# A memory-attention and gating kernel on one core: the spatial weight is loaded first, and the written order is new

## The chip, the core and the metric

The kernel runs on one core of a Trainium2 chip. Five engines work side by side: TensorE (PE, with its weight loads shown as PEld), VectorE (DVE), ScalarE (ACT), GpSimd (POOL) and SyncE (SP), which here issues every DMA. The metric is the device time of one execution in microseconds.

## The reference

Two parts are joined. The first is attention over a small memory, for 8 batches and 8 heads, 576 positions, 64 dimensions and 32 memory slots; the second is a gated feed-forward layer whose gate mixes positions.

```python
a = softmax(phi, axis=positions)            # [B, H, 576, 32]
k_m, v_m = a^T k, a^T v                     # [B, H, 32, 64]
attn = softmax(q k_m^T / 8) ; x = attn v_m  # heads side by side: [B, 576, 512]
h = relu(x @ w_in)                          # [B, 576, 1024]
u, v = h[..., :512], h[..., 512:]
v_n = (v - mean(v)) / sqrt(var(v) + 1e-6)
v_s = w_spatial @ v_n + b_spatial           # mixes the 576 positions
out = (u * v_s) @ w_out                     # [B, 576, 512]
```

All data is float32 except `w_in` and `w_out`, which arrive as 64-bit floats and are decoded on the chip.

## The kernel before, in words

The kernel is a set of small generators, one for each kind of work, and each `yield` ends a step. The string `START` is the written order: each letter takes one step of the generator that it names, so the string alone sets the order of the instructions on every engine (`manual_schedule`, PE, DVE, ACT, POOL and SP). A digit picks the part (a tile or a weight), `*n` repeats, one prime is one batch ahead, and `>` moves on to the next batch.

- `P` loads `phi` and takes its softmax; `K` loads `k` and `v` and forms the two memories (tile `kvm`, then `vmn`, `tv`, `vT`); `Q` loads `q` and transposes it (`tq` in batch 0, `qT` from `q_sb` later); `S` makes the scores and their softmax (`sc`, `sm`, and the transposed result `at` split into a high and a low part `ah`, `al`).
- `M` multiplies `vT` with a half of `w_in` (`mp`, split into `mh`, `ml`); `V` makes a block of `v` and normalizes it (`pv`, `vr`, `st`, `few`, `vh`, `vl`); `U` makes `u` (`pu`); `G` is the spatial product and the gate (`ps`, `g`, `gh`, `gl`); `O` is the last product (`po`, `o`) and the store.
- Weights: `D` loads `w_in` (`load_win`, D1 its v half in four pieces E00 to E11, D0 its u half in two pieces L0 and L1) and `E`/`L` decode it (`decode`: one ACT, one POOL or ACT, one DVE instruction a piece, into `win_sb`); `X` does the same for `w_out` (`raw_out`); `W` loads `w_spatial` and its bias (`w_sb`, `w_rem`, `b_sb`), `T` transposes it (PE tiles `wt`, `wr`) and splits it into `wth` and `wtl` (and `ws`).

A weight load can be held: `hold` (line 194) lets POOL copy one element of a tile that has landed into the buffer that the load will write, so that the DMA behind it starts only when that landing is in. `HOLD` (line 98) names which landing each load waits for: E0 for `k`, E1 for `v`, L0 for E00, L1 for E10 and W for E11. So the loads of the start run `phi`, `q`, `k`, `v`, then the v half of `w_in`, then its u half, and the spatial weight last.

[...] The first batch's products need the decoded v half of `w_in` (`mp` line 711), `ah` and `al`; the first `pv` (line 744) needs all of these; the first `ps` (line 864) needs the normalized blocks and the transposed spatial weight.

Of the kernel before, what the change touches and what calls it, by code (L numbers as in the profile page):

```python
# [17 lines left out]
PSUM = bass.MemoryType.PSUM  # L18

START = """  # L20
    P*4 Q P*4 K D1 P*3 Q P*4 Q P*2 K*4 K1 K Q D1 K Q*2 K*2 D1 K D1 K E0*2 Q D1*2 E1 Q S Q S Q*2 S
# [4 lines left out]
    V0 X0 V4 V1 K' V2 V4*2 V1 X2 P' T4 U3 V2 K' V4 V1 V3 T4 P' G2 V4 T4 U0 X1 Q' U0 G0 V3 P' P'' K'
    Q' U0 K' U1 V2 S V3 V2 V4 K' Q' G2 G0 V2 G2 B U1 P'' K'' V3*2 G0 K' V4 K'*2 V3 V4*2 P''*2 X2 K'
    V4 K'' P'' G0 X3 U1 Q' K' P'' G0*2 P'' G0 G2*2 S' G3 G2 K' X1 G0 G1 P'' X2 P'' S'*3 X3 G1 S' G3
    G2 P'' G0 G2 X2 G1 T2 U1 G0 S' G2 P'' S' P'' G3 G1 G3 P'' M1' M0' L1 S' G1 X3 K''*2 G2 G1 M1'*2
    G1 S' P''*2 Q'' X3 M0' G3 G1 S' Q'' G3 K'' M1' X2 X3 O0 O3 T4 S' X2 S' G3 S' K'' O1 G3 S' M0'  # L30
    S' X3 S' O3 P''' M1' S'*2 M1' P''' O0 G1 O1 S' M0' V1' M0' P''' O3 S' V1' V2' V0' P'''*2 M0'
    V2' U1' O1 K''*2 V1' V0' V2' P''' Q'' U1' O0 V4' K''*2 V2' U0' Q'' V2' P''' V2' K'' P''' V0'
    P''' O2 G1 K'' Q'' V0' U1' V3' U0' V2' K''' O2 U3' V1' V4' P''' K''' P''' U2' V0' U3' S' V1' M0
    X1 V4' U2' K'' K1 U1' V0' Q'' V4' P''' V1' V0' X2 P''' S'' T3 V3' O2 U3' P''' V4' M0'' K''' G3
    V3' O3 V1' S''*2 O1 P''' U0' V4' U2' K''' U2' S'' U3' G3 M1'' M1' U0' S'' V3'*2 S'' K''' V4'*2
    V3' K''' G1' T0 P'''' G1' S'' M0'' G0' V4' G1' Q''' K''' G0' K''' V4' M0' V3' Q''' K''' M1''
    K'''' S'' G0' G1' G0' M1'' S'' G3' G1'*2 G3' P'''' G2' G0' S'' M1'' P'''' G1' G2' G3' S''*2 G2'
    G3' P'''' G0' S''*2 M1'' G2' G0' M0'' G0' S'' G0' S'' P'''' S'' G1' T1 X3 G1' G0' S'' G2' G1'
    P'''' G2'*2 M1 O3' S'' P'''' Q''' O1' G3' M0'' V0'' G3' V0'' K''' G3' S'' G2' V4'' G2' V4'' O0'
    O2 G2' G3' O0 > P''' O0 V1' V4'*2 V3' O2 K'' Q'' O0 P''' O2 G3 Q'' G3 V1' O3 K'' V0' V1' O4 M0'  # L40
    O2 V2' U1' K''' V0' U3' V1' X0 M1' U3' V0' U1' O1 U2' U0' K'' V0' P''' V1' P''' U0' V3' U3'
    P''' V1' U1' O2 O4 V0' V2' O3 P''' Q'' O0 U2' M0'' U0' P''' U1' U0' V1' V2' V3' M0' U3' S''
    K'''*2 P''' M1'' V4' O1 V2' V4' V3' U2' V2' O4 G1' S''*2 U2' V3' S'' V4' M0''*2 O3 V3' G1' M0''
    O1 O4 V3' M0'' G0' V4' S'' V2'*2 P'''' O0 G1' S'' V4'*2 M1'' G1' G0' S'' G0' G1' M1'' G0' G3'
    K''' S''*2 G3' P'''' O1 > Q'' S' G2 G0 G1 S' O4 P''' G2 G0 S' G1 P''' K'' G2 P''' G0 S' G0 G1
    K'' G0 G2 G3 S'*2 K''' G3 P''' K'' S'*2 G0 K'' M1' S' O0 G3 U3' G1 K'' G3*2 G1 Q'' G2 M1' G2 S'
    V1' G2 S' V4' P''' O1 V0' G2 V4' G3 U3' O0 K'' V0' O2 Q'' V0' V1' P''' O3 G3 U3' V3' K'' V1'
    P''' O0 U1' O2 V0' Q''*2 U1' U3' Q'' M0' V1' V0' P''' K'' U0' G3 P''' V4'*2 U0' V4' V0' P''' O1
    V0' U0' G2 U2' O2 U2' V3' U1' V1' K''' V2' V3' U2' O1 V1' O3 S'' P''' V1' O0 P''' M0'' M1'' S''
    U2' V3' Q''' V2' Q''' K''' P''' V4' U0' S S''*2 U1' K''' S'' V3' V2' O3 M1' O0 M0'' G0' M0''  # L50
    K''' V4'*2 S'' V2' M1'' V3' V2' M1'' V3' V2'*2 M0'' G0' G1' G0' V4'*2 G2 K''' G1'*2 O1 G1' M0''
    S' S'' G1' K''' S'' G0'*2 G3' P'''' G0' P'''' G2'*2 S'' G1'*2 P'''' G2' G3' G0' S'' M1'' S''
    G1' S'' G1' G0'*2 O4'' G3' P'''' K''' G2' G3' G1' G0' S'' G2' G3' S'' P'''' M1'' K''' O3' S''
    G3' G2' G3' O2 P'''' O1' S''*3 O4' U1'' S'' G3' V1'' G2' M0'' O0' O3 S'' G2' K'''' V1'' V0''*2
    U1'' O0' V1'' V0'' P'''' V4'' P'''' O3' V4'' K''' V4'' U1'' V1'' O1' V0''*2 Q''' O0' V0''
    U0''*2 Q''' U3'' G3' U3'' V4'' G3' V1'' Q''' G2' V0'' U1'' V4'' V2'' O3' U0'' V1'' K''' U3''
    O1' P'''' K'''' U3'' V2'' Q''' G2' U2'' V4'' O0' V4''*2 O1' K''' V3''*2 V1'' O2' P'''' U2''*2
    K''' O2' P'''' S'' V4'' O4' U2'' S''' U0'' V2'' V3'' V2'' M0''' K'''' S''' V3'' M1''' K''''
    M1'' S''' O4' O2' O3' G1'' G0'' V2'' G1'' G0'' S''' V3'' M0''' P'''' V2'' V3'' P''''*2 S'''*2
    M0''' M1'''*2 V2'' V4'' M1''' P'''' S''' G1'' G0'' V3'' M1''' S''' O4' O1 > S'' P'''' S'' G1'  # L60
    G0' G3' G1' S'' Q''' G1' G0' G1' S'' G3' S'' G0' S'' G3' K'''' P'''' G3' S''*2 G1' P'''' K'''
    G2' M0'' G1' G0'*3 G2' S'' G0' O1 G2'*2 G3' S'' P''''*2 K''' S'' O2 G3' S'' G1' G3' V1''*2
    P'''' K'''' V4'' K''' G2' V0'' M0'' G2' U3''*2 M1'' K''' P''''*2 V0'' Q'''*2 U0'' G3' K''' Q'''
    V4'' P'''' U3'' V4'' G2' V0'' K''' V0'' U0'' Q''' K''' O2' G2' O2' O0' V0'' K''' V0'' V4'' O0'
    V4'' K''' G2' V2'' V3'' O1' V1'' O3' Q''' O2' U3'' U2'' V4''*2 O1' V1'' V0'' P'''' U0'' U1'' O0
    > V3' O0 V1' G3 O3 U0' V1' V3' P''' G2 P''' U1' U2' P''' O1 S'' M1'' V1' V2' V4' U1' V2' S'' O2
    O3 V4' U2' M0' U2' S'' U1' V2'*2 M0'' M1'' V2' P''' K''' M1'' K''' S'' G0' V2' V3' G0' M0'' V3'
    G1' G3 Q''' S'' M0'' V4' S'' M1'' G0' S'' M0'' V3' O0 M1'' P''' G1' S'' V3' G1'*2 G0' S'' G1'
    S'' M0'' Q''' S'' G1'*2 S'' G0' S'' G3'*2 S''*2 G0' S''*2 G0' G3' G2' G0' G2' S''*2 G1' Q'''
    K''' G3' G2'*2 V0'' V2'' G0' V0'' O1 K''' G0' V0'' G1' O3' V2'' U1'' G1' G2' K''' G2' K''' O2'  # L70
    S'' G3'*2 V1'' V0'' G2' Q''' V0''*2 K''' U1'' G2' V4'' U3'' O0' V1'' G3' V4'' G2' U1'' V0''
    V4'' K''' O1' G3' V4'' V2'' V1'' O0' U3'' G2' O1' O0' O2' V4'' U3'' V4'' U1'' V3'' K''' Q'''
    V4'' O4' V4'' S' G3' V4''*2 O2' G3' O1' V3'' O4' U2'' K''' V4'' V1'' O3 O4' U2'' O0' V3'' U0''
    V2'' Q''' V1'' U2'' U0'' V2'' O1 V3'' U3'' V3'' O3' S''' K''' U0'' M0''' S''' U2'' U0'' V3''
    M1''' K''' O3' S''' V1'' M0''' O0' V1'' S''' M1''' V2'' S''' M0''' G2'' G1'' G2'' M1'''*2 S'''
    V2'' S''' M1''' G1'' G0'' V3'' G0'' S''' G0'' S''' M0''' G1'' G0''*2 G2'' S'''*2 G1'' G3'' G0''
    G2'' S''' U1'' G3'' S''' M0''' G0'' S''' O1' O0 > G3' S'' G0' S'' G1' S''*2 G0' G3' G0' U2''
    S'' V1'' G1' U3' G2' G1' S'' G1'*2 G2' V1'' V0'' G1' V3'' G3' U2'' V0'' O2 V3'' V0'' Q'' V0''
    U1'' V0'' V1'' V4'' U1'' V1'' G3' G2' U0'' U3'' V1'' G3' U2''*2 V0'' O1' V1'' U0'' U3'' V0''
    G3' V4''*3 V2'' G2' V4'' U1'' O3' U0'' G3' U0'' V2'' V1'' O3' U3'' O1' O2' V3''*2 O0' V2'' V4''  # L80
    G0'' V4'' V2'' V3'' V4'' G0'' U1'' V4'' O4 V2'' G3' U3'' V2'' V3'' G1'' V2'' G0'' O2' V4'' G1''
    V3'' G3'' G0'' G1'' G0'' G1'' O3 G3'' G2' O1' O3' G2' U0' O0' G2'' G1'' G3'' G0'' G1'' G2''
    G3'' O2' G1'' G2'' O0' G1'' G0'' O1' G0'' G2'' G1'' G0''*2 G3'' G1'' G2''*2 G3'' O4'' O2'
    G2''*2 O0' G3'' O3'' G3'' O3'' O0'' O1'' O1 > G2' O0' O3 > G3 O3 G2 O1 G3 O4 O0 O2 O1 O2 O3 O4
# [901 lines left out]
```

## Time and profile before

| | us |
|---|---|
| time of the kernel, median of 3 runs | 415.3 (414.23 to 415.58) |
| the profiled execution | 416.39 |
| its span, from the first to the last instruction | 414.6 |
| PE busy | 388.7 (94% of the span) |
| DVE busy | 278.7 (67%) |
| ACT busy | 221.6 (53%) |
| POOL busy | 96.0 (23%) |

The page shows PE busy in nearly every slice after the first quarter; its open slices lie at the start and at the very end. The transfers of the start are `phi` of one batch (576 KB), `q`, `k` and `v` (1152 KB each), `w_spatial` (1152 KB and a rest of 144 KB), `w_in` (four pieces of 512 KB, two of 1024 KB) and `w_out` (four of 512 KB).

### The profile page before, as it was taken

How to read it: one execution, taken by the hardware profiler on the slowest of the kernel's cores; microseconds unless marked ns; L12 is line 12 of the kernel's file. 1: busy time of each engine (PE TensorE's matmuls, PEld its weight loads, DVE VectorE, ACT ScalarE, POOL GpSimd, SP SyncE). 2: the span in 40 equal slices, each digit the busy share in tenths (PEclk: the TensorE clock that was granted, in tenths of full speed). 3: DMA queues.
4: the chain of work that ended last, by engine and by line, in shares of the span. 5: the costliest groups of instructions: out<-in, count | busy, mean ns of one | idle time of the engine just before them, and what ended most of it. 6: DMA issues, size and time to landing. Idle time of an engine off the chain costs nothing.

```text
span 414.6 us, 9446 instructions
## 1 busy us (share of the span) xinstructions
PE 388.7 (94%) x3903; PEld 336.5 (81%) x3903; DVE 278.7 (67%) x547; ACT 221.6 (53%) x455; POOL 96.0 (23%) x188
## 2 busy tenths in 40 slices
...
GB/s 300 318 306 304 195 284 197 73 278 27 73 154 227 51 52 154 242 60 134 44 298 2 26 64 129 293 20 149 69 2 0 28 82 22 1 2 25 54 49 101
DMA packets 85758, 50.69 MB, mean 122 GB/s; under 512 B 66194, under 2 KB 70290, under 8 KB 85716
## 3 DMA queue, kind: packets, MB, share of 16 engines
...
q14 instruction: 12, 0.10, 0.1%
HBM read 40.65 MB, written 9.44 MB: 121 GB/s over the span
## 4 chain that ended last, share of the span: by engine, by line
PE 76%; DMA 8%; DVE 6%; SPq 3%; POOL 2%; issue 1%; ACT 1%; DVEq 0%; POOLq 0%; ACTq 0%
PE ps L864 26%; PE po L901 22%; PE pu L828 10%; PE pv L744 9%; DMA kv_sb<-in_v_dram 3%; PE kvm L460 3%; PE mp L711 3%; SPq L516 2%; DMA q_sb<-in_q_dram 2%; DMA w_sb<-in_moe_w_spatial_dram 2%; PE sc L645 2%; DMA raw<-in_moe_w_in_dram 1%; DVE gl L885 1%; POOL raw L225 1%; SPq L448 1%
## 5 line engine op out<-in xcount | busy, mean ns | idle before, releaser
L864 PE MATMUL ps<-wth,vh 128*128 128x288 f32 x256 | 56.8, 302 | 0.1
L864 PE MATMUL ps<-wth,vl 128*128 128x288 f32 x256 | 55.0, 296 | 0.8 <-DVE vl L806 0.8
L864 PE MATMUL ps<-wtl,vh 128*128 128x288 f32 x256 | 54.7, 295 | 0.0
L901 PE MATMUL po<-woh,gl 128*128 128x512 f32 x128 | 50.3, 393 | 1.7 <-DVE gl L885 1.7
L901 PE MATMUL po<-woh,gh 128*128 128x512 f32 x128 | 51.0, 398 | 0.0
L901 PE MATMUL po<-wol,gh 128*128 128x512 f32 x128 | 50.1, 392 | 0.0
L883 ACT CAST gh<-g 128x512 fp32r<-128x512 f32 x32 | 19.6, 618 | 48.1 <-DVE g L877 41.7
L864 PEld LDWEIGHTS ps<-wth,vh 128*128 128x128 f32 x256 | 41.5, 189 | 3.6 <-DVE sm L656 1.1
L864 PEld LDWEIGHTS ps<-wth,vl 128*128 128x128 f32 x256 | 41.1, 188 | 1.1 <-DVE vl L806 1.1
L864 PEld LDWEIGHTS ps<-wtl,vh 128*128 128x128 f32 x256 | 41.2, 188 | 0.0
L789 DVE BATCH_NORM_STATS2 st<-vr 128x6 f32<-128x512 f32 (+1 forms) x40 | 27.2, 679 | 18.8 <-ACT vr L786 18.6
L828 PE MATMUL pu<-ah,mh 128*128 128x288 f32 x128 | 38.5, 301 | 0.2 <-ACT u L837 0.2
L801 ACT ACTIVATE vr<-vr,few 128x512 f32<-128x512 f32 (+1 forms) x40 | 32.0, 814 | 11.2 <-POOL few L796 11.1
L828 PE MATMUL pu<-al,mh 128*128 128x288 f32 x128 | 37.8, 295 | 0.0
L828 PE MATMUL pu<-ah,ml 128*128 128x288 f32 x128 | 37.7, 294 | 0.0
L877 DVE TENSOR_TENSOR g<-u,ps 128x288 f32<-128x288 f32 x64 | 26.9, 443 | 14.4 <-PE ps L864 13.6
L806 DVE TENSOR_TENSOR vl<-vr,vh 128x512 fp32r<-128x512 f32 x32 | 21.8, 682 | 20.9 <-ACT vh L804 20.7
L907 ACT COPY o<-po 128x512 f32<-128x512 f32 x36 | 20.9, 588 | 21.9 <-PE po L901 19.7
L695 POOL CAST ar<-ah 128x128 fp32r<-128x128 f32 x7 | 3.5, 494 | 122.5 <-ACT ah L688 122.5
L792 POOL TENSOR_SCALAR few<-few 128x1 f32<-128x1 f32 (+1 forms) x40 | 10.1, 252 | 93.7 <-DVE few L790 78.6
L786 ACT ACTIVATE vr<-pv 128x512 f32<-128x512 f32 x32 | 19.1, 600 | 21.8 <-PE pv L744 19.6
L901 PEld LDWEIGHTS po<-woh,gl 128*128 128x128 f32 x128 | 24.0, 188 | 7.8 <-DVE gl L885 2.6
...
## 6 DMA issues: line engine op xcount, KB each, us to landing
...
raw_out<-in_moe_w_out_dram SPq DMA_DIRECT2D x4, 512.0 KB, 10.2
```

The costliest lines, as they stand in the source:

```text
L460: nc.tensor.matmul(kvm[r][32 * j : 32 * j + 32], phi_sb[halves[r], j, i, :], kv_sb[halves[r], j, :, i * D : (i + 1) * D], start=(i == 0), ...
L744: nc.tensor.matmul(pv, x[:, r, cs], m[:, r, DM:DFF], start=(n == 0), stop=(n == 5))
L786: nc.scalar.activation(vr, pv, AF.Relu)
L789: nc.vector.bn_stats(st6, vr)
L801: nc.scalar.activation(vr, vr, AF.Identity, bias=sh, scale=rs)
L806: nc.vector.tensor_tensor(vl[:, st, :], vr, vh[:, st, :].bitcast(F32), op=ALU.subtract)
L828: nc.tensor.matmul(pu[hf], m[:, r, cs], a[:, r, at[hf]], start=(r == 0 and n == 0), stop=(r == 1 and n == 2),)
L864: nc.tensor.matmul(ps[hf], a, w[:, hf * HALF : (hf + 1) * HALF], start=(n == 0), stop=(n == len(ops) - 1),)
L877: nc.vector.tensor_tensor(g[:, at], u[:, dt, at], ps[hf], op=ALU.mult)
L883: nc.scalar.copy(hi, x)
L901: nc.tensor.matmul(po, a, w, start=(n == 0), stop=(n == 11))
L907: nc.scalar.copy(o, po)
```

## The change

`w_spatial` (both parts) is issued as the very first transfer and held for nothing; `phi`, `q`, `k` and `v` follow. Holds are moved: E1 is held for the landing of the spatial weight (long in by then), L0 for `v`, L1 for E00, and the first two loads of `w_out` get a hold of their own (X0 for E11, X1 for L00). The string `START` is written anew up to its last batches (the piece behind the last but two `>` is the same). All instructions stay, but for one POOL copy that goes and two that come.

```diff
 START = """
-    P*4 Q P*4 K D1 P*3 Q P*4 Q P*2 K*4 K1 K Q D1 K Q*2 K*2 D1 K D1 K E0*2 Q D1*2 E1 Q S Q S Q*2 S
+    W*2 P*2 T4 T1 P*2 Q K P*4 T0 W P*2 Q T1 Q P*3 Q T4*2 T0 Q T1 P*2 T4 D1 T4 Q T1 Q P T4 T1 K T0
...
-HOLD = {"E0": "k", "E1": "v", "L0": "E00", "L1": "E10", "W": "E11"}
+HOLD = {"E0": "k", "E1": "W", "L0": "v", "L1": "E00", "X0": "E11", "X1": "L00"}
...
     def prepare_out(b, j):
         raw = two.tile([P, 1, 2 * DM], I32, tag="raw_out", name="raw_out")
+        if f"X{j}" in HOLD:
+            hold(raw[0:1, :, 0], HOLD[f"X{j}"])
         nc.sync.dma_start(raw[:, 0], w_out[j * P : (j + 1) * P].bitcast(I32))
...
-        hold(w_sb[0:1, 0, 0:1].bitcast(I32), HOLD["W"])
-        yield
+        if "W" in HOLD:
+            hold(w_sb[0:1, 0, 0:1].bitcast(I32), HOLD["W"])
+            yield
         nc.sync.dma_start(w_sb, w_spatial[0:SM].rearrange("(i p) s -> p i s", i=NI))
+        state["landed", "W"] = w_sb[0:1, 0, 0:1].bitcast(I32)
         yield
```

SP, the start of the program, before (`in_moe_w_in` is `w_in`, and so on):

```order
L333 DMA phi_sb<-in_phi_dram 128x4x288
L534 DMA q_all<-in_q_dram 128x4x576
L375 DMA kv_sb<-in_k_dram 128x4x576
L375 DMA kv_sb<-in_v_dram 128x4x576
L206 DMA raw<-in_moe_w_in_dram 128x1024 x4
L206 DMA raw<-in_moe_w_in_dram 128x2x1024 x2
L266 DMA w_sb<-in_moe_w_spatial_dram 128x4x576
L268 DMA w_rem<-in_moe_w_spatial_dram 64x576
L333 DMA phi_sb<-in_phi_dram 128x4x288
```

and in the changed kernel, at the same place:

```order
L271 DMA w_sb<-in_moe_w_spatial_dram 128x4x576
L274 DMA w_rem<-in_moe_w_spatial_dram 64x576
L339 DMA phi_sb<-in_phi_dram 128x4x288
L540 DMA q_all<-in_q_dram 128x4x576
L381 DMA kv_sb<-in_k_dram 128x4x576
L276 DMA b_sb<-in_moe_b_spatial_dram 2x576
L381 DMA kv_sb<-in_v_dram 128x4x576
L208 DMA raw<-in_moe_w_in_dram 128x1024 x3
L208 DMA raw<-in_moe_w_in_dram 128x2x1024
L208 DMA raw<-in_moe_w_in_dram 128x1024
L208 DMA raw<-in_moe_w_in_dram 128x2x1024
L454 DMA kv_sb<-in_k_dram 128x4x576
```

1296 KB of spatial weight now stand ahead of `phi`, one 1024 KB piece of the u half has passed the last piece of the v half, and the next batch's `k` follows the weights at once.

PE, from the start of the program to the first products of `k`, before:

```order
L343 MATMUL mt_105<-ident,mx 128x128
L352 MATMUL mb_116<-ident,cmb 128x128
L544 MATMUL tq_121<-ident,q_all 128x128 x4
L386 MATMUL kvm_0_0_135<-kv_sb,phi_sb 32x64
L386 MATMUL kvm_0_1_136<-kv_sb,phi_sb 32x64
```

and in the changed kernel:

```order
L299 MATMUL wt_110<-ident,w_sb 128x128 x4
L299 MATMUL wr_111<-ident,w_rem 128x64
L349 MATMUL mt_125<-ident,mx 128x128
L299 MATMUL wt_131<-ident,w_sb 128x128 x4
L299 MATMUL wr_132<-ident,w_rem 128x64
L358 MATMUL mb_139<-ident,cmb 128x128
L550 MATMUL tq_143<-ident,q_all 128x128 x4
L550 MATMUL tq_153<-ident,q_all 128x128 x4
L299 MATMUL wt_158<-ident,w_dup 128x128 x4
L299 MATMUL wr_159<-ident,w_rem_dup 128x64
L550 MATMUL tq_176<-ident,q_all 128x128 x4
L392 MATMUL kvm_0_1_186<-kv_sb,phi_sb 32x64
```

Three of the five sets of spatial transposes and two more sets of `q` transposes now stand ahead of the first product of `k`.

DVE, from the end of the first softmax of the scores to the split of the first products, before:

```order
L606 TENSOR_TENSOR sm<-sm,rsum 128x640
L229 SCALAR_TENSOR_TENSOR win_sb<-raw 128x512
L229 SCALAR_TENSOR_TENSOR win_sb<-raw 128x2x512
L186 TENSOR_TENSOR al<-at_417,ah 128x128x4
L186 TENSOR_TENSOR al<-at_434,ah 128x128x4
L186 TENSOR_TENSOR al<-at_442,ah 128x128
L186 TENSOR_TENSOR wtl<-wt_456,wth 128x512
L186 TENSOR_TENSOR ml<-mp_1_0_446,mh 128x512
L186 TENSOR_TENSOR wtl<-wr_457,wth 128x64
L186 TENSOR_TENSOR ml<-mp_1_1_447,mh 128x512
```

and in the changed kernel:

```order
L612 TENSOR_TENSOR sm<-sm,rsum 128x640
L231 SCALAR_TENSOR_TENSOR win_sb<-raw 128x512
L231 SCALAR_TENSOR_TENSOR win_sb<-raw 128x2x512
L188 TENSOR_TENSOR al<-at_457,ah 128x128x4
L188 TENSOR_TENSOR al<-at_477,ah 128x128x4
L188 TENSOR_TENSOR ml<-mp_1_0_493,mh 128x512
L188 TENSOR_TENSOR al<-at_508,ah 128x128
L188 TENSOR_TENSOR ml<-mp_1_1_494,mh 128x512
```

The two splits of the spatial weight have left this place; the rest stands in nearly the same order.

## Rows read from the trace of the kernel before

**Rows 1.** Windows by stage: stretch, length, busy PE/PEld/DVE/ACT/POOL (instructions), clock, DMA share, GB/s.

```profile
0.00:37.44 37.44, 20.94 (x440) 15.69 (x440) 21.73 (x43) 16.57 (x32) 16.36 (x26) 0.86 0.92 312
37.44:52.61 15.17, 15.10 (x226) 11.87 (x226) 14.84 (x30) 13.34 (x27) 9.79 (x13) 1.00 1.19 208
52.61:65.36 12.75, 10.01 (x74) 9.17 (x70) 9.11 (x18) 8.82 (x19) 9.23 (x14) 1.00 0.89 282
65.36:90.00 24.64, 24.18 (x318) 19.66 (x318) 24.28 (x45) 11.58 (x23) 4.71 (x4) 1.00 0.72 176
90.00:400.00 310.00, 307.52 (x2806) 271.36 (x2805) 208.44 (x414) 168.31 (x351) 55.97 (x134) 1.00 0.39 86
```

**Rows 2.** Waits of PE, 0 to 37.4 us: waiter, releaser, total us, times, longest.

```profile
PE tv L437 <- ACT vmn L434: 4.0, 1, 4.0
PE kvm L386 <- issue: 2.1, 1, 2.1
```

**Rows 3.** Timelines, waits on landings: start, us, instruction, [idle before <- releaser].

```profile
5.29 0.69 DVE L322 TENSOR_TENSOR half<-phi_sb 128x512 f32<-128x512 f32 x1 [5.29 <-DMA phi_sb<-in_phi_dram]
14.30 0.18 POOL L194 COPY raw<-kv_sb 1x2 int32<-1x2 int32 x1 [2.50 <-DMA kv_sb<-in_v_dram]
29.05 1.10 ACT L220 ACTIVATE raw<-raw 128x1024 f32<-128x1024 f32 x1 [2.96 <-DMA raw<-in_moe_w_in_dram]
```

**Rows 4.** Timeline of PE in the first 45 us.

```profile
11.42 2.27 PE L386 MATMUL kvm<-kv_sb,phi_sb 64*32 64x64 f32 x144 [1.70 <-DMA kv_sb<-in_k_dram]
14.06 1.95 PE L544 MATMUL tq<-ident,q_all 128*128 128x128 f32 x8
32.08 1.96 PE L711 MATMUL mp<-win_sb,vT 64*32 64x512 f32 x16
33.97 0.97 PE L293 MATMUL wt<-ident,w_sb 128*128 128x128 f32 x4
37.44 0.50 PE L744 MATMUL pv<-mh,ah 128*128 128x512 f32 x1
42.90 0.60 PE L293 MATMUL wt<-ident,w_dup 128*128 128x128 f32 x4
```

**Rows 5.** Timelines of DVE and ACT, from the first softmax to the split of `mp`.

```profile
18.68 0.69 DVE L588 TENSOR_REDUCE rmx<-sc 128x16 f32<-128x512 f32 x1
27.29 1.94 DVE L229 SCALAR_TENSOR_TENSOR win_sb<-raw 128x512 int32<-128x512 int32 x2
31.99 1.67 DVE L186 TENSOR_TENSOR al<-at,ah 128x512 fp32r<-128x512 f32 x3 [2.76 <-ACT ah L628]
35.46 0.59 ACT L720 CAST mh<-mp 128x512 fp32r<-128x512 f32 x1
36.20 0.68 DVE L186 TENSOR_TENSOR ml<-mp,mh 128x512 fp32r<-128x512 f32 x1
```

**Rows 6.** Windows, granted clock, around its low stretch.

```profile
28.00:30.00 2.00, 0.00 (x0) 0.00 (x0) 1.22 (x1) 0.95 (x1) 0.91 (x1) 0.50 0.98 374
35.00:36.00 1.00, 1.00 (x7) 0.70 (x8) 0.40 (x1) 1.00 (x3) 0.00 (x0) 1.00 0.99 393
```

**Rows 7.** The chain that ended last, in order of time: start, us, piece.

```profile
24.29 9.10 DMA w_sb<-in_moe_w_spatial_dram
46.02 9.26 DMA q_sb<-in_q_dram
99.03 1.38 PE pv L744 x6
```

**Rows 8.** Waits of DVE, 37.4 to 100 us.

```profile
DVE qT L525 <- DMA q_sb<-in_q_dram: 1.8, 1, 1.8
```

**Rows 9.** Waits of PE, 37.4 to 100 us.

```profile
PE ps L864 <- DVE t L814: 1.1, 1, 1.1
PE ps L864 <- DVE vl L806: 0.8, 1, 0.8
PE tk L492 <- ACT vmn L488: 0.8, 1, 0.8
```

More of the change, by code (lines that the diff above doesn't have):

```diff
@@ L26 @@
[L26 to L84, printed above, removed]
@@ new lines @@
+    P' V1 U3 X1 U3 V2 S V1 X0 V1 U2 P' V4 U2 V3 P' K' V3 X0 U3 K' P'*2 T3 U2 G0 V2 V4 X1 G2 X0 X2
+    U1 V3 V4*2 P' V2 K' P'' U3 U0 V2 G0 V4 G2 V3 U1 V4 B K' S K' Q'*2 V2 V4*2 V2 X1 V4 Q' G0 L0 Q'
+    K'' U1 K' V4 P'' G2 K'' P'' G0 P'' G2 G0 P'' X2 P'' U1 G0 K' G1 G0 G2 K' P'' G1 P''*2 T2 K' G2
+    K' X2 G0 X2 G2 S' P'' G1 G2 X3 G2 S'*2 G2 G0 K' G1 Q'' S' P'' G0 G3 G1 S' G3 X2 G3 G1 G3 M0'
+    M1' S' G1 P'' S' P'' G3 S' G3 S' P''*2 K'' G1 M1' X3 G3 K'' X3*2 O0 S' G3 M1' O3 O1 X2 K'' S'
+    M0' Q'' X3*2 O1 M1' S'*2 G3 S' M0' S' M1' O0 S' K'' S' K'' S' M1' P''' K''' O0 M0' O3 S' K''
@@ new lines @@
+    V2' P''' O3 M0'*2 K'' X2 V1' U1' V2' U1' V1' V2'*2 P'''*3 V1' V2' S' P''' V0' K'' P''' G1 V4'
+    P''' V0' P''' U0' Q'' V2' Q'' V1' V0' O1 K''' U1'*2 V4' Q'' U3' V3' K'' V2' V1' P''' Q'' V4'
+    V0' V1' U3' U0' U2' K'' G3 K'' V1' P'''*2 V4' P''' O2 U0' U2' U3' O2 V0' V4' V0' U3' L1 V3'*2
+    T3 V4'*2 S'' K''' G1 M0'' U2' V3' U0' U2' P''' M1'' S'' T1 K''' S'' V0' O2 S''*2 V4'*2 P'''
+    K''' M0' M0'' O3 M1' M0'' O1 O2 K''' M1'' G1' V3' M1'' G1' G0'*2 V3'*2 K''' M1'' Q''' O0 G0'
+    G1' V4' S'' G0' S'' G0' G1' S''*2 G2' G0' G1' K''' P'''' T0 Q''' G2' G1' K''' X1 G3' M0'' S''
@@ new lines @@
+    G0' G1' S'' K''' S''*2 G2'*2 S'' G1' G3'*2 G0' G1' M1'' P'''' G1' S'' G2' G0' S''*2 O0' P''''
+    S'' G0' M0 S'' O3' G2' Q''' K'''*2 G2' G3' P'''' K'''' G2' V0'' S'' V4'' P'''' G3' P'''' G3'
+    V4'' O1' G3' V1'' P'''' V4'' G3' V1'' O3' K'''' O0' O3' M0'' M1 V0'' V1'' O2' V3'' G3' V1''
+    Q''' O2' V4'' G3' O0' V1'' O4' V2'' U1'' V0''*2 V1'' Q''' P'''' V3'' P'''' O0' O2' U0''*2 O1'
+    V4'' G2' U1'' U3'' V0'' O3' K''' V0'' Q''' V1'' P'''' U0'' O1' V4'' U3'' G2' O2' P'''' U0''
+    U2''*2 M0'' V3'' P'''' V0'' O4' V4'' V2'' S' V4''*2 P'''' M0''' S''' U3'' V2'' U1'' M1'' Q''''
@@ new lines @@
+    K'''' U2''*2 U1'' S''' K1 > K''' V4' U3' O4 M0'' V3' S'' P''' M1'' M0'' V2' S'' V2' M0'' O0 V3'
+    S'' V3' G1' V2' G1' V3' M0'' V2' P''' S'' O4' S'' G0' G1' K''' M1'' P'''' M1'' P'''' G1'*2 G0'
+    X0 G0' M1'' S'' O1 G1' G0' S'' K''' G2' M1'' G1'*2 S'' G2' G0'*2 S''*2 G1' K''' G0' G2'*2 G3'
+    S'' G3' S'' K''' G0'*2 S'' G1' S'' P'''' S'' G0' S'' G3' G2' P'''' O4 S' S'' G2' K''' O1 > O0
+    K''' S' G3 P''' G3 V0' U1'*2 G3 O2 G3 V1' G2 Q'' G3*2 P''' O4'' Q''*2 V0' G2 V1' K'' O0 U3' O1
+    P''' O1 Q'' K'' V0'*2 U3' V4' V0' G2 V1' K'' O0 P''' K'' U1' V1'*2 V2' P''' U1' P''' O3 G3 O1
@@ new lines @@
+    O2 V4'*2 U3' V4' P''' V0' Q'' U2' U3' U2' G2 K''' V2' V3' V4' V0' O3 M1' U0' V1'*2 P''' V2' V4'
+    O0 P''' U2' U0' O2 S'' O1 M1'' V3' U0' V3' U0' K''' O3 M0'' K''' U2' V2' G1' K'''' S'' G0' V4'
+    S'' X3 V3' G1' M1'' V4' M1'' P''' S'' M1'' V4' V3'*2 S'' M0' V2' G0' V2' O0 M1'' P''' S'' V3'
+    K''' V4' V2' G1'*2 M0''*2 G0' S'' K''' M0'' G1' P'''' S'' G0' S''*2 G1' K''' G3' K''' G0' G2'
+    P'''' G3' K''' G1' G0' M0'' O1 S'' G0'*2 G3' G2' G1' G2' G3' O3' S''*2 G0' S'' O2 P'''' S'' G0'
```

42 lines of the change are left out of this document (37 added, 5 removed).

## The prediction, made before the changed kernel was run

> **What bounds the kernel now.** I read the busy shares by stage first. From 90 to 400 us PE is busy 307.52 of 310.00 us [rows 1]: TensorE is the bound there, and only 2.5 us are open. The open time is at the start. Up to 37.44, when the first product of the gate (`pv`) starts, PE is busy 20.94 us, so 16.5 are open. From 37.44 to 52.61 it is full; from 52.61 to 65.36 it has 10.01 of 12.75; from 65.36 to 90 it has 24.18 of 24.64 while DVE has 24.28, so two engines are full there. As the change keeps the PE instructions, the time can only move with the open time: before 37.44, in the 2.74 us behind 52.61, and in what a new order opens or closes later.
>
> Then the waits. Before 37.44 the largest one inside the work is 4.0 us of PE for `vmn` from ACT, beside one of 2.1 us in which PE waited for nothing that the profile shows ("issue") [rows 2]. ACT could not make `vmn` because it stood behind the decoding of the last piece of `w_in`, which waited until 29.05 for its landing [rows 3]. Only then come `mp` at 32.08 and `pv` at 37.44 [rows 4]. The spatial weight is issued at 24.29 and lands 9.10 us later [rows 7]; its transposes fill the place between `mp` and `pv` [rows 4]. Behind 52.61 PE waits 0.8, 0.8 and 1.1 us for the last normalized blocks and for `vmn` of the next batch [rows 9], and DVE has waited 1.8 us for that batch's `q` [rows 8], which lands at 46.02 + 9.26 = 55.28 [rows 7]. Normalization stands behind this transpose on DVE.
>
> **The transfers.** `phi` (576 KB) was in at 5.29, `v` (4032 KB in all) at 14.30 [rows 3]: 3456 KB in 9.01 us, an estimate of 384 KB/us. `k` (2880 KB) at 11.42 [rows 4] lies on that line. 1296 KB in front cost 3.4 us: `phi` lands at 8.7, `q` 11.7, `k` 14.8, `v` 17.7. Because E1 now waits for something long landed, the loads run on without a gap: E00 19.0, E01 20.4, E10 21.7, the first u piece 24.4, E11 25.7, the second u piece 28.4 (before: 29.05), the next batch's `k` 31.4, its `phi` 32.9, two pieces of `w_out` 35.6, its `v` 38.6. Before, the stretch from the spatial weight's landing (33.39) to that of `q` (55.28) moved 3904 KB besides `q`: 10.2 us at the same rate, which leaves 11.7 for `q`, whose rows are short. So `q` lands at about 50.3, 5 us earlier. What holds this back is small: the two new holds stand on POOL behind decoding, and the holds end before the queue is empty.
>
> **The first softmax chain.** It moves later. `mb` stands at 12.1 (3.4 later, and one set of transposes between). Then PE has 8 `tq` at 1.95, a set of spatial transposes at 0.97 and 0.3 for its rest, and 4 more `tq` at 1.0 [rows 4], so that the first `kvm` starts at 16.5 and not at 11.42, although `k` is in at 14.8. Between `kvm` and the scores there are now 4 `tq` less ahead of the transposed memory, worth 0.9. So the first maximum on DVE, before at 18.68 [rows 5], comes 5.1 - 0.9 = 4.2 later, at 22.9. The softmax took 18.68 to 27.29, 8.6 us [rows 5], and has one more decode (0.6) and a small split (0.1) in it now: done at 32.2. Before, DVE then had room: it waited 2.76 us for `ah` [rows 5]. This room is what pays for the delay.
>
> **To the first `pv`.** The decode of E11 ends at 32.8, the last set of `at` at 33.4. `vmn` is no longer last: with 72 products of `v` behind the scores, PE is through at about 26.5, or 28.6 with the 2.1 us of issue, and ACT, behind E11's decode, makes `vmn` at 30. `mp` takes 1.96 [rows 4], to 35.4; then `mh` 0.6 and `ml` 0.6 [rows 5], with a last `al` of 0.3: `pv` starts at 36.9, against 37.44. I take a gain of 0.5. At full clock `mp` would take half, a gain of 1.5; if the issue wait falls into the chain where nothing covers it, a loss of 1.6.
>
> **The spatial transposes.** Two of five sets remain near this place, one of them in PE's wait for `vmn` and `at`, one beside the splits. The set that stood behind `pv_2` at 42.90 goes from the full stretch: 0.60 and its rest, 0.8 with what follows [rows 4]. The three sets that went to the front run while PE waits for `phi` and `q`; without that cover each costs 1.3 (the one ahead of `kvm` does, and is in the 16.5). DVE and ACT lose a split and a copy each per set behind 37.44, three sets before, two now, with the bias copy about 2 us each, so neither is later than PE. The first `ps` comes at 52.61 - 0.5 - 0.8 = 51.3.
>
> **The stretch behind 52.61.** `q` at 50.3 is in before DVE reaches its transposes (before 53.6, now about 52), so the 1.8 go. ACT counted in its new order, piece by piece at 0.4 to 0.8 us from the first `pv`, ends the last normalized block at about 58.4, before at 62.8; PE alone would reach the product that needs it at 51.3 + 9.3 = 60.6. So the 2.74 us go as far as PE is not held elsewhere. I take 2.3 of them; bounds 0 and 2.74. What is late next is PE itself, and from 65 on DVE, which is as far ahead.
>
> **The later batches.** The string is new there too. All work is the same; PE has 2.5 us open in 310 [rows 1] and can lose them or get as many more. The trace can't show it: bounds 2.5 either way, and I take 0, since the rows show PE full whatever stood next to it. The two POOL copies are one element each, 0.18 us by the row at 14.30 [rows 3], in a POOL that is not full.
>
> **A rule on the clock.** The granted clock is 0.50 at 28 to 30 us, with PE idle, and back at 1.00 at 35 [rows 6], behind 4 us of unbroken work; the same four transposes take 0.97 then and 0.60 later [rows 4]. So the 12 products of `pv_0` and `pv_1` (six take 1.38 at full clock [rows 7]) run at full clock in the sum. [...] By rows I give that 0.12: the engine works nearly without a break from 30 on.
>
> **The sum**, against the profiled execution (416.39, of which 414.6 is span and 1.8 lies around it; it is 1.1 above the median of 415.3): 0.5 + 0.8 + 2.3 = 3.6 us. Profiled 412.8; median 411.7.
>
> **The rivals.**
> - The start is gained, the rest not: DVE is full from 65 to 90 [rows 1] and sets the time there, so the closed waits open again a little later, and the median is 415.3 - 1.3 = 414.0, or up to 415.5 if a new order costs 1.5 among the later batches. For it: DVE's 24.28 of 24.64. Against it: what DVE does behind 37.44 has shrunk, and it is earlier by as much as PE. Chance 0.20.
> - Slower: `phi`, `q`, `k` and `v` are 3.4 late and the softmax chain is the new bound. [...] From a `pv` later than 38.7 on, the 0.8 and part of the 2.3 no longer pay. With `pv` at 39.5 and the later waits kept: 415.3 + 2.1 - 0.8 = 416.6. For it: 5.1 us that `kvm` is late, and only 0.5 us of margin left at `pv`. Against it: the gaps in the chain were counted from the slow pace already. Chance 0.10; with the clock rule's case (415.3 + 1.5 = 416.8, or less where the waits behind 52.61 still close) 0.20 in all.
> - More than forecast: `mp` at full clock, all 2.74 and some of the 2.5 us closed: 5 to 6.5 us, 409 to 410.3. Chance 0.15.
>
> **How the numbers follow.** The forecast has 0.45, with its own range 410.3 to 413.5. To hold eight in ten the range takes in the better case to 408.9 and most of the first rival to 415.6. A difference of 0.3% is 1.25 us, about what a measurement can tell from no change. Faster by more: 0.45 + 0.15, and half of the first rival and the mild end of the clock case, 0.70. Within: 0.15. Slower: 0.15.
>
> **What would show it.** Right: `phi` landing near 8.7 and the last piece of `w_in` near 28.4; the first `kvm` near 16.5; DVE without its wait for `ah` near 32; `pv` near 37, the first `ps` near 51; `q` landing near 50; PE idle below 1 us between 51 and 65; 90 to 400 open by about 2.5 us again. Wrong: `pv` later than 38.7; a clock of 0.50 while `pv` runs; a new wait of PE on DVE between 60 and 100 as long as those that went; or PE open by over 5 us behind 100.

## The result, and the profile after

The change made the kernel slower: 421.02 us median (419.37 to 421.51) against 415.44, a ratio of 1.0123 with a 95% interval of 1.0075 to 1.0171. The forecast was 411.7 with a range up to 415.6. The profiled execution after took 421.15 us with a span of 419.4, against a span of 414.6 before: 4.8 us to explain.

First the windows of the changed kernel by stage (stretch, length, busy PE/PEld/DVE/ACT/POOL, granted clock, DMA share, GB/s), with four short ones for the clock at the end. They answer to [rows 1] and [rows 6].

```profile
0.00:36.40 36.40, 21.07 (x445) 16.38 (x446) 22.52 (x45) 17.29 (x35) 15.73 (x26) 0.91 0.95 335
36.40:51.94 15.54, 15.51 (x226) 12.00 (x226) 14.55 (x29) 12.53 (x26) 9.99 (x16) 1.00 0.98 176
51.94:61.00 9.06, 8.47 (x61) 7.53 (x56) 7.74 (x13) 8.05 (x18) 7.80 (x11) 1.00 0.82 292
61.00:76.78 15.78, 15.48 (x284) 13.00 (x284) 15.32 (x32) 7.59 (x15) 2.13 (x2) 1.00 0.83 163
76.78:90.00 13.22, 10.02 (x35) 7.78 (x33) 10.15 (x18) 3.81 (x8) 1.45 (x1) 0.74 0.70 224
90.00:297.36 207.36, 207.16 (x2104) 181.29 (x2102) 147.71 (x290) 120.45 (x250) 45.14 (x101) 1.00 0.48 109
297.36:303.60 6.24, 3.85 (x48) 3.65 (x48) 3.70 (x5) 0.33 (x1) 0.00 (x0) 0.75 1.05 155
303.60:400.00 96.40, 95.88 (x642) 86.53 (x642) 55.84 (x113) 46.81 (x97) 12.58 (x34) 1.00 0.08 27
80.00:83.00 3.00, 0.06 (x1) 0.00 (x0) 2.97 (x5) 0.33 (x1) 0.00 (x0) 0.85 0.82 248
84.00:86.00 2.00, 2.00 (x7) 1.52 (x6) 0.52 (x2) 0.00 (x0) 0.00 (x0) 0.50 0.99 363
89.00:90.00 1.00, 1.00 (x6) 0.82 (x5) 0.28 (x1) 0.00 (x0) 0.00 (x0) 1.00 0.00 0
301.00:303.00 2.00, 2.00 (x10) 2.00 (x10) 0.06 (x1) 0.00 (x0) 0.00 (x0) 0.50 1.52 137
```

The reader is to see two short stretches that are out of line, and nothing else. Up to 76.78 PE is open 16.3 us. The 2.74 us behind the first `ps` [rows 1] have shrunk to 0.59. From 90 to 297 PE is open by 0.20 in 207 us. But from 76.78 to 90.00 it is open by 3.20 us, and from 297.36 to 303.60 by 2.39, and in each of these stretches the granted clock falls to 0.50: the first time before the wait is over (0.85 on average from 80 to 83), the second time behind it. It stays there for a while although PE works without a break by then (0.50 with PE busy 2.00 of 2.00 us, from 84 to 86 and from 301 to 303).

Next the timeline of PE in the changed kernel (start, length, instruction, [idle before <- releaser]). The first lines answer to [rows 4].

```profile
15.33 1.87 PE L392 MATMUL kvm<-kv_sb,phi_sb 64*32 64x64 f32 x144
33.71 1.34 PE L717 MATMUL mp<-win_sb,vT 64*32 64x512 f32 x16
36.40 0.48 PE L750 MATMUL pv<-mh,ah 128*128 128x512 f32 x1 [0.42 <-ACT ah L634]
...
76.78 0.50 PE L907 MATMUL po<-woh,gh 128*128 128x512 f32 x1
...
79.67 0.39 PE L907 MATMUL po<-woh,gl 128*128 128x512 f32 x1
83.27 0.79 PE L907 MATMUL po<-woh,gh 128*128 128x512 f32 x1 [3.21 <-DVE ml L188]
...
299.75 0.84 PE L466 MATMUL kvm<-kv_sb,phi_sb 64*32 64x128 f32 x34 [2.39 <-issue]
```

And the two places of before that answer to the second half of it, PE's timeline of the kernel before:

```profile
77.88 2.25 PE L460 MATMUL kvm<-kv_sb,phi_sb 64*32 64x128 f32 x144
...
80.53 0.48 PE L901 MATMUL po<-woh,gh 128*128 128x512 f32 x1
```

The same `kvm` product of the next batch starts at 77.88 before and at 74.60 after: at this point the changed kernel is 3.3 us ahead. So the start delivered nearly what was forecast (3.6), and the loss is all behind it. Single executions differ here: with the old start this product comes at 77.72 and 76.16 in two more traces (experiments 3 and 6), with the new start at 74.28 to 75.26 in four more (1, 2, 4 and 5). The means, 77.25 and 74.73, are 2.5 us apart.

What PE waited for from 36.4 to 100 us, the changed kernel (waiter, releaser, total, times, longest), beside [rows 9]:

```profile
PE po L907 <- DVE ml L188: 3.2, 1, 3.2
PE pv L750 <- ACT ah L634: 0.4, 1, 0.4
PE pu L834 <- ACT u L843: 0.4, 1, 0.4
PE ps L870 <- DVE t L820: 0.3, 1, 0.3
```

The waits of [rows 9] (1.1, 0.8, 0.8) have become 0.3, and a new one of 3.2 us stands in their place: a product of `po` that needs nothing of `ml` waits for `ml`. What it needs is a PSUM bank, one of the eight buffers of the pool `ps1`. `po_1` takes over the bank of `mp_0_0` of the next batch, whose last reader is the split `ml`, and DVE is in no hurry with it. DVE's timeline in the changed kernel:

```profile
22.94 0.69 DVE L594 TENSOR_REDUCE rmx<-sc 128x16 f32<-128x512 f32 x1 [1.83 <-PE sc L579]
...
78.15 0.63 DVE L891 TENSOR_TENSOR gl<-g,gh 128x512 fp32r<-128x512 f32 x1
78.70 1.80 DVE L259 TENSOR_TENSOR wol<-raw_out,woh 128x512 fp32r<-128x512 f32 x1
80.42 1.35 DVE L681 TENSOR_TENSOR sm<-sm,rsum 128x1152 f32<-128x1152 f32 x1
81.80 0.84 DVE L690 STREAM_TRANSPOSE aT<-sm 128x288 f32<-128x288 f32 x2
82.56 0.65 DVE L188 TENSOR_TENSOR ml<-mp,mh 128x512 fp32r<-128x512 f32 x1
```

ACT had written `mh`, the other input of this `ml`, by 77.06. `ml` runs at 82.56 only because the written order puts `wol`, `sm` and two `aT` ahead of it. In the kernel before, `po_1` takes a bank that ACT frees, and PE goes through its first 24 products of `po` with 0.40 us of waiting at most.

**Where the 4.8 us are.** PE stands idle for 26.3 us after (419.4 less 393.1 busy) and for 25.9 before (414.6 less 388.7): nearly the same. The start won 3.1 us of idle time (19.4 up to 80.53 before, 16.3 up to 76.78 after), and what lies behind took 3.5 back: the two new waits cost 5.6, and older waits that closed gave back some 2.1. The rest, 4.4 us, is in PE's busy time, for the same 3903 matmuls: the products behind the two waits ran at half clock. From 83.27 to 88.96, with a mean clock of 0.50, PE did 12 `po` and 2 `kvm` in 5.69 us, where the next 12 `po` took 2.8: 2.7 us lost. From 300.52 to 304.25, with a mean of 0.54, it did 14 `ps` and 2 `kvm` in 3.73, where such work takes 2.0 later: 1.7 lost. Each wait cost 0.7 to 0.8 of its length again.

### The profile page after: what moved, and what is told of

Same layout as the page of the kernel before. It is cut to its first block, busy times and chain, and to the rows that moved or that the text cites. A ratio compares the mean times of both kernels' runs of the same rounds, so it can differ in the third digit from the quotient of the medians.

```text
span 419.4 us, 9436 instructions
## 1 busy us (share of the span) xinstructions
PE 393.1 (94%) x3903; PEld 340.9 (81%) x3903; DVE 280.5 (67%) x547; ACT 221.2 (53%) x455; POOL 94.8 (23%) x189
## 3 DMA queue, kind: packets, MB, share of 16 engines
q1 hardware_dynamic: 85716, 50.10, 46.4%
## 4 chain that ended last, share of the span: by engine, by line
PE 81%; DVE 9%; ACT 3%; issue 2%; POOL 2%; DMA 2%; SPq 0%; DVEq 0%; ACTq 0%; POOLq 0%
PE ps L870 27%; PE po L907 24%; PE pu L834 10%; PE pv L750 9%; PE kvm L466 3%; PE mp L717 3%; PE sc L651 2%; DMA phi_sb<-in_phi_dram 2%; DVE win_sb L231 1%; POOL raw_out L227 1%; DVE qT L531 1%; PE pv L766 1%; PE pv L758 1%; DVE half L328 1%; POOL few L799 1%
## 5 line engine op out<-in xcount | busy, mean ns | idle before, releaser
L907 PE MATMUL po<-woh,gh 128*128 128x512 f32 x128 | 52.1, 407 | 3.2 <-DVE ml L188 3.2
L907 PE MATMUL po<-wol,gh 128*128 128x512 f32 x128 | 51.2, 400 | 0.0
L812 DVE TENSOR_TENSOR vl<-vr,vh 128x512 fp32r<-128x512 f32 x32 | 23.3, 727 | 14.9 <-ACT vh L810 14.8
L907 PEld LDWEIGHTS po<-woh,gh 128*128 128x128 f32 x128 | 24.7, 193 | 8.7 <-DVE ml L188 3.6
L701 POOL CAST ar<-ah 128x128 fp32r<-128x128 f32 x7 | 5.0, 707 | 118.3 <-ACT ah L694 118.3
```

What stands on the lines that cost most here:

```text
L812: nc.vector.tensor_tensor(vl[:, st, :], vr, vh[:, st, :].bitcast(F32), op=ALU.subtract)
L907: nc.tensor.matmul(po, a, w, start=(n == 0), stop=(n == 11))
```

## The experiments

**1. The split moved ahead.** Two steps of the string, one of them the `ml` of the bank, are written ahead of the step of `w_out` that makes `wol`. In the order of the instructions this moves one DVE instruction and nothing on PE or ACT.

```diff
-    ... O0 S' G3 M1' O3 O1 X2 K'' S'
-    M0' Q'' X3*2 O1 M1' S'*2 G3 S' M0' S' M1' O0 ...
+    ... O0 S' G3 M1' O3 O1 M0' M0' X2 K'' S'
+    Q'' X3*2 O1 M1' S'*2 G3 S' S' M1' O0 ...
```

> The changed kernel (421.0 us) with one DVE instruction moved: the ml of mp_0_0 of batch 1 (0.65 us), the last reader of the PSUM bank that po_1 takes at 80 us, now stands ahead of wol (1.80), sm L681 (1.35) and two aT, not behind them. PE's and ACT's order is untouched. Theory A (the 3.21 us in which PE stands still at 80-83, and the clock of 0.50 behind it that makes 24 po take 8.4 instead of 5.6 us, come from this place in DVE's order): the wait on ml goes; po_1's second matmul can still wait for wol until about 81.2, so 0 to 1.3 us stay; if the clock stays at 1.00 all 4.5 to 6 us come back: 415.0 to 416.5; if the short rest still brings the clock down 2 to 3 us less. Rival (DVE is full from 65 to 90 and sets the time there; any order only moves the wait): the 3 us show up again at al or den ahead of the next pv, and the time stays at 419.5 to 421.5.

Measured: 415.39 us median, 5.6 less than the changed kernel's 421.02; against before a ratio of 1.0022 (0.9993 to 1.005). The two medians were taken at different times; by their ratios to the before of the same time (1.0123 and 1.0022) the gain is some 4.2 us. DVE's timeline and the window of the place, of this kernel:

```profile
78.38 0.68 DVE L188 TENSOR_TENSOR ml<-mp,mh 128x512 fp32r<-128x512 f32 x1
78.97 1.21 DVE L259 TENSOR_TENSOR wol<-raw_out,woh 128x512 fp32r<-128x512 f32 x1
```

```profile
77.00:92.00 15.00, 14.81 (x73) 12.26 (x71) 13.27 (x28) 7.92 (x18) 3.88 (x8) 1.00 0.62 215
```

`ml` is done at 79.06, PE no longer waits, and the clock stays at 1.00. Theory A holds and the rival falls: DVE has all its old work in this stretch, only in another order, and the wait doesn't come back further on. That more than the 3.2 us of the wait return, with the clock at 1.00 in this window, shows that the slow clock belonged to the wait.

**2. Two loads of `q` moved back.** The stall at 297 has no releaser in the trace ("issue"). Two of the last batch's four loads of `q_sb`, issued by SP at 291.30, are written behind the store that goes at 297.22.

```diff
-    ... U2'' O3' V2'' Q'''' V3''*2 V2'' M0''' S''' P''''
+    ... U2'' O3' V2'' V3''*2 V2'' M0''' S''' P''''
...
-    ... S'''*4 K'''' Q'''' G0'' S'''*2 ...
+    ... S'''*4 K'''' Q'''' Q'''' G0'' S'''*2 ...
```

> The changed kernel (421.0 us) with one SP step moved: the first two of the four q_sb loads of the last batch (rows of 128 bytes, issued at 291.3 us) now go behind the store at 297.2, in one row with the other two; all other engines' order is untouched, and the first reader (qT, 318 us) is far. Theory F1 (the PE stall without a releaser at 297.4-299.8, 2.39 us in the middle of a kvm product, is PE waiting for a 16 KB instruction packet that stands behind these small rows in the DMA engines): stall at 297 under 0.8 us, clock stays 1.00 behind it, 4 us back: 416.5 to 417.5. Theory F2 (a packet of instructions simply takes longer to come than the kvm stretch takes to use one up, whatever else the DMA engines do): stall stays at 2 to 3 us, 420.5 to 421.5.

Measured: 416.36 us median, 4.7 less than 421.02 (1.0047 of before, 1.0021 to 1.0074; by the ratios some 3.2 less). Between the two profiled spans lie 4.5 us: 4.1 are the stall and the slow clock behind it, 1.2 come from a shorter slow stretch at 80 us (last section), and 0.7 were lost before that. The window of the place in this kernel, to be compared with 13.61 of 16.00 and a clock of 0.89 in the same window of the changed kernel:

```profile
290.00:306.00 16.00, 16.00 (x282) 13.76 (x282) 11.01 (x21) 9.07 (x20) 2.52 (x6) 1.00 0.69 111
```

The DMA queues show why (queue, kind: packets, MB, share of 16 engines). In the changed kernel the packet of instructions is in the half microsecond from 296.5, just where the short rows of `q` end; from 293.0 to 296.5 the queue had moved 4109 packets under 512 bytes and no instruction packet:

```profile
q8 instruction: 1, 0.02, 20.2%
q1 hardware_dynamic: 48, 0.01, 15.3%
```

With the loads moved back, the same packet is there in the half microsecond from 294.0, alone:

```profile
q8 instruction: 1, 0.02, 17.9%
```

PE went on at 299.75 in the changed kernel, about 3 us behind the packet. With the packet at 294.0 no stall is seen. F1 holds: the packet of instructions (of which queue q8 has 30, 0.49 MB in all, in an execution) came later when rows of `q` were in the queues, by 2.5 us on the two timelines, which lie some 0.5 us apart there. No row names the engine that a packet is for; that these hold PE's instructions is read from PE's going on 2.2 to 3.3 us behind one of them at each stall of this kind.

**3. The same suspect put into the kernel before.** The kernel before has this product at 295.15 without a visible stall (2.74 us for 144 matmuls; the 144 at 77.88 took 2.25, so half a microsecond may be hidden in it). Its last loads of `q` are moved the other way, so that their rows are under way when the packet is due.

```diff
-    S'' M0'' Q''' S'' G1'*2 ...   ... G2'*2 S''*2 G1' Q'''
-    K''' G3' ... K''' G0' V0'' G1' O3' V2'' ...
+    S'' M0'' S'' G1'*2 ...   ... G2'*2 S''*2 G1'
+    K''' G3' ... K''' G0' V0'' G1' Q''' Q''' O3' V2'' ...
```

> The kernel before (415.1 us) with the second pair of the last batch's q_sb loads moved behind the store at 289.4 us, so that its rows of 128 bytes are under way at 294, when PE's 16 KB instruction packet is fetched in the kvm product (that product took 2.74 us there, without a visible stall). The two qT steps that read them first move along; nothing else moves. Theory F1 (the packet stands behind such rows): a stall of 1.5 to 3 us in or next to that kvm product at 295-298, and a slow clock behind it of up to 1.6 us: 416.8 to 419.5. F2 (the rows have nothing to do with it): no stall over 0.8 us there, 414.5 to 415.8.

Measured: 416.65 us median against 415.96, a ratio of 1.0033 (0.9991 to 1.0076): by the time alone it is open whether it is slower, and the median lies between what the two theories had. The trace is not open. PE's timeline of this kernel, and its DMA queues in the half microsecond from 293.5:

```profile
293.83 1.77 PE L460 MATMUL kvm<-kv_sb,phi_sb 64*32 64x128 f32 x110
296.75 0.84 PE L460 MATMUL kvm<-kv_sb,phi_sb 64*32 64x128 f32 x34 [1.15 <-issue]
```

```profile
q1 hardware_dynamic: 207, 0.09, 149.6%
q8 instruction: 1, 0.02, 20.6%
```

A stall of 1.15 us has appeared inside the product, of the kind that F1 says and shorter than the 1.5 to 3 expected: here the rows ended at about 294, and the packet came with their end, some 3 us ahead of PE's going on. It is in the half microsecond in which the product starts (293.83); in the kernel before it is in the one from 294.0, about a microsecond ahead of the start (295.15). The clock stayed at 1.00 behind this shorter wait, so the expected second price was not paid. The same product stalls in experiments 1 and 6, whose loads of `q` stand as in the changed kernel; PE's timelines of the two:

```profile
293.93 0.86 PE L466 MATMUL kvm<-kv_sb,phi_sb 64*32 64x128 f32 x34 [2.18 <-issue]
```

```profile
299.68 0.84 PE L461 MATMUL kvm<-kv_sb,phi_sb 64*32 64x128 f32 x34 [1.52 <-issue]
```

Behind the 2.18 us pairs of `ps` took 0.68 us up to 297.76 and 0.43 from 298.39 on, with a mean clock of 0.89 from 290 to 306; behind the 1.52 it stayed at 1.00. How long such a stall is for a given delay of the packet stays open.

**4. Both moves.** The diffs of 1 and 2 in one kernel.

> Both moves of the two runs before in one kernel. Theory A with F1: 421.0 less 4.5 to 6, less 4: 411.0 to 412.5, which is what the forecast of the change had (411.7) and faster than the kernel before (415.4). A with F2: 415 to 416.5. Rival of A with F1: 416.5 to 417.5.

Measured: 411.85 us median (410.79 to 412.31), a ratio of 0.9940 to before (0.9912 to 0.9969) and 9.2 us less than the changed kernel. Windows of this kernel:

```profile
77.00:92.00 15.00, 14.65 (x93) 11.94 (x77) 13.28 (x29) 7.95 (x18) 3.15 (x7) 1.00 0.59 215
290.00:306.00 16.00, 16.00 (x206) 15.01 (x191) 13.90 (x26) 5.75 (x12) 0.00 (x0) 1.00 0.76 109
92.00:290.00 198.00, 197.87 (x2013) 174.12 (x2019) 141.81 (x278) 114.84 (x239) 43.56 (x96) 1.00 0.47 110
```

No stretch behind the start is out of line any more. With two causes taken away the time is what the forecast had for the change, and this kernel is faster than both others. That the number agrees so well is in part luck: of the 4.6 us between the spans (414.6 and 410.0), 3.2 lie up to the first `po` (80.53 and 77.30) and 1.4 behind it, where the forecast had 3.6 and 0, and the profiled execution of before is 1.1 above its median.

**5. The new start with the old order behind it.** The changed kernel's first 305 of 1571 steps, up to about 73 us, and then all that is left in the order of before.

```diff
-    X2 G0 X2 G2 S' P'' G1 G2 X3 G2 S'*2 G2 G0 K' G1 Q'' S' P'' G0 G3 G1 S' G3 X2 ...
+    X2 G0 X2 G2 S' P'' G1 G2 X3 G2 S'*2 G2 G0 K' G1 Q'' S' P'' G0 G3 X3 S' G3 S'*2 ...
```

> The changed kernel's first 305 of 1571 written steps (the start and batch 0 up to 73 us) and behind them all that is left in the order of the kernel before. Theory A (the start's 3.4 us are real and stand at 77 us; it is the new order behind that loses them): 411.5 to 413. Rival (an earlier PE only runs into DVE at 80-90 in whatever order): 414.5 to 416.

Measured: 412.55 us median, a ratio of 0.9973 (0.9945 to 1.0001). The waits of PE in this kernel from 80 to 400 us are:

```profile
PE po L907 <- DVE gl L891: 1.2, 1, 1.2
PE pu L834 <- ACT u L843: 0.6, 1, 0.6
PE kvm L466 <- issue: 0.4, 1, 0.4
```

The median lies where theory A has it, though the interval just takes in no change. The 1.2 us for `gl` is a wait that the kernel before has too (1.3). In the trace the first `po` is at 77.02 against 80.53 before, and behind it lie 333.7 us against 334.1: the start keeps its gain with either order behind it, once that order has no hole.

**6. The old start with the new order behind it.** The other way round: 305 steps, holds and loads of before, then the changed kernel's order.

> The kernel before in its first 305 written steps (its loads, its holds and its start), and behind them the changed kernel's order. Theory A (the order behind the start loses the time, with any start): PE comes to the po at 80 us 3.4 us later than in the changed kernel and DVE 1.3 later, so that the wait on ml is about 1.1 us instead of 3.2, with or without a slow clock behind it (0 to 2.8); the stall at 297 and the slow clock stay (4.0); what the kernel before lost behind 200 goes (2.5): 417.5 to 421. Rival (the order behind the start is harmless, the changed kernel's start and its rest only don't fit together): 414.5 to 416.

Measured: 421.55 us median (418.99 to 423.11), a ratio of 1.0129 (1.0052 to 1.0207). That is 0.5 above theory A's upper end, by four runs alone, and not for the reason given: the wait on `ml` was expected to shrink to 1.1 us. PE's timeline of this kernel:

```profile
81.21 0.39 PE L902 MATMUL po<-woh,gl 128*128 128x512 f32 x1
85.18 0.68 PE L902 MATMUL po<-woh,gh 128*128 128x512 f32 x1 [3.58 <-DVE ml L187]
```

It grew to 3.58. I had taken DVE to be at its place 1.3 us later than in the changed kernel and PE 3.4; here the first `po` is at 78.34 instead of 76.78, 1.6 later, and DVE's `wol` at 80.62 instead of 78.70, 1.9 later. The hole is a matter of the order alone and moves along with both engines. The stall at 297 was expected to stay with its slow clock (4.0); in the profiled execution, the fastest of the four, it was 1.52 us with the clock at 1.00 (experiment 3). What the slower runs lost beyond that is not shown.

**7. The old holds.** The kernel of experiment 4 with the holds of before.

```diff
-HOLD = {"E0": "k", "E1": "W", "L0": "v", "L1": "E00", "X0": "E11", "X1": "L00"}
+HOLD = {"E0": "k", "E1": "v", "L0": "E00", "L1": "E10"}
```

> The kernel with both moves (411.85 us) with the holds of the kernel before: E1 waits for v, L0 for E00, L1 for E10, and the loads of w_out for nothing. Theory A' (the holds only shift landings that have room: the gain of the start comes from the spatial weight being in early and its transposes being out of the full stretch): 411.3 to 412.5. Rival (the holds are part of the gain: without them w_out shares the DMA engines with the last pieces of w_in and the first mp comes later): 412.8 to 414.5.

Measured: 412.27 us median, 0.9925 of before (0.9898 to 0.9952), against 0.9940 with the new ones in experiment 4. The moved holds make no difference that can be told by the time. In the one trace with the old holds `pv` starts at 38.12, in the five with the new ones at 36.20 to 37.15, so that up to a microsecond at the start may be theirs.

**8. The spatial weight first, and nothing else.** The kernel before with the two loads of `w_spatial` as the first transfers and without their hold; all other steps stand in the old order.

```diff
-    P*4 Q P*4 K D1 ...
+    W*2 P*4 Q P*4 K D1 ...
...
-HOLD = {"E0": "k", "E1": "v", "L0": "E00", "L1": "E10", "W": "E11"}
+HOLD = {"E0": "k", "E1": "v", "L0": "E00", "L1": "E10"}
```

> The kernel before (415.1 us) with the spatial weight's two loads as the very first transfers and its hold gone; the written order of everything else and the other holds are those of before. Theory A'' (the transfer alone is worth little, since the transposes still stand in the full stretch and k, v and w_in now land 3 us later while the order of the start still meets them in the old order): first pv at 37.5 to 39 instead of 37.4, the 1.8 us wait for q_sb smaller: 414 to 416. Rival (the early landing is the whole gain): 411.5 to 413.

Measured: 419.22 us median, a ratio of 1.0072 (1.0035 to 1.0108): worse than either theory. PE's timeline of this kernel:

```profile
14.84 2.27 PE L390 MATMUL kvm<-kv_sb,phi_sb 64*32 64x64 f32 x144 [1.70 <-DMA kv_sb<-in_k_dram]
34.14 1.96 PE L715 MATMUL mp<-win_sb,vT 64*32 64x512 f32 x16
39.53 0.50 PE L748 MATMUL pv<-mh,ah 128*128 128x512 f32 x1
```

`k` lands 3.4 us later, the scores behind it too, and the four sets of transposes still stand between `mp` and `pv`: `pv` starts at 39.53, 2.1 us behind [rows 4], and the first `po` at 83.48, 3 us behind. This is the second rival of the prediction, with its `pv` at 39.5, in the kernel that has the transfer and not the order; the median is 3.3 us above before, where that rival had 1.3. I expected `pv` at 37.5 to 39 and a smaller wait for `q_sb` to pay for it. The first was too hopeful. The second did not pay: DVE's wait for `q_sb` is gone, but PE waits 1.29 us for `vl` at 64.61 and 1.36 for `t` at 66.50, longer than in [rows 9], and pairs of `ps` take 0.67 and 0.69 us from 67.51 on and 0.43 again from 71.69, with a mean clock of 0.88 from 60 to 70 and 0.95 from 70 to 80.

## Why the prediction was wrong, step by step

**The transfers: right up to `v`, late behind it.** POOL's timeline of the changed kernel, the two copies that wait for `k` and `v`:

```profile
14.84 0.18 POOL L196 COPY raw<-kv_sb 1x2 int32<-1x2 int32 x1 [6.73 <-DMA kv_sb<-in_k_dram]
17.82 0.18 POOL L196 COPY raw<-kv_sb 1x2 int32<-1x2 int32 x1 [2.68 <-DMA kv_sb<-in_v_dram]
```

14.8 and 17.7 were forecast; `phi` was in at 8.8 (8.7). But the last piece of `w_in`, issued at 20.98, landed 9.3 us later, at 30.3 and not at 28.4, and the next batch's `phi` was issued only at 30.72, behind a wait of SP for PE's `kvm`: the loads did not run on without a gap. Why the pieces came late is open. The last `q_sb` was in at 49.5 (50.3), and `pv` was not later for it.

**The softmax chain and `pv`: right.** The first maximum on DVE stands at 22.94 (22.9). The first `kvm` came at 15.33 and not at 16.5, which changed nothing, since the scores came as forecast. `pv` started at 36.40 (36.9). The issue wait grew from 2.1 [rows 2] to 3.7 us and was covered: the chain that ended last runs through DVE there. The second rival took `pv` at 39.5, 2.1 us later than before; no run with the new start shows that (36.20 to 37.15 in five traces, 38.12 in the one with the old holds), and experiment 8, at 39.53, shows when it does happen.

**The spatial transposes and the stretch behind `ps`: right in sum.** The first `ps` came at 51.94 where 51.3 was forecast: the transposes have left the stretch, but six products of `pu` stand ahead of `ps` in their place, and take as long. The stretch behind it lost 0.59 us instead of 2.74, and no wait for `q_sb` was left. PE was 3.3 us ahead at the `kvm` of the next batch, against a forecast of 3.6.

**What is late next: wrong.** "What is late next is PE itself, and from 65 on DVE, which is as far ahead." DVE was 3.5 us ahead at `t` (61.1 against 64.6), but only 1.3 at `sm` (80.42 against 81.76), and that is not what mattered. The prediction's own sign of being wrong came: a new wait of PE on DVE between 60 and 100, 3.2 us, as long as those that went (2.7). PE waited for an instruction that DVE could have run 4 us earlier. I had compared how much DVE has to do with how much time it has. A wait comes from what stands ahead of one instruction in its queue, and the new order moved `wol` and `sm` ahead of a split that frees a PSUM bank. The first rival had the right place (65 to 90) and the wrong mechanism, a full engine; experiment 1 leaves DVE's work as it was and wins 4.2 to 5.6 us.

**The later batches at 0, with bounds of 2.5 either way: wrong, by the size and by a mechanism that was not in it.** The bounds were made of PE's open time before. The new order closed most of what was open between 200 and 290, and opened 2.39 us at 297 through a transfer that no wait in the profile names: the packet of instructions behind rows of `q`. The trace of before had the sign, an unexplained issue wait of 2.1 us [rows 2], which I called a thing that might fall into the chain at the start and did not ask about elsewhere. It looks the same: such a packet is in the quarter microsecond from 22.25, and PE goes on at 24.65 (in the changed kernel 27.25 and 29.78). There the queues were busy with long rows (6 of 152 packets under 512 bytes from 20 to 22 us before), so that short rows may not be needed; no experiment tests it.

**The clock: priced at the wrong place.** It was weighed for the start and nowhere else. A slow clock through `pv` had a chance of 0.12 and a loss of 1.5 us (416.8); no run shows that loss, and in the changed kernel the clock was 1.00 from 36.40 to 51.94, while `pv` ran. The rows show that the clock fell with waits of 3.21 and 2.39 us and cost 2.7 and 1.7 us beyond them. At 80 us it went to 0.50 some 2 us into the wait and was back at 88.9; at 297 it went there 0.8 us behind the end of the wait and was back at 304.0. The clock's price here, taken along with the bound of 2.5 us of new waits, would have made that bound 4 to 4.5 us and the upper end of the range 2 us higher, which is still short of what came at both places together (3.2 + 2.7 and 2.4 + 1.7).
